# Moving spatial weight tiles and the bias out of the last pass of a two-layer attention and gMLP kernel, and lending it idle PSUM banks

## The chip, the cores and the metric

The kernel runs on one core of a Trainium2 chip. The metric is the device time of one execution in microseconds (us), lower is better.

## The reference, cut to what matters

Two layers, each an attention with 32 query heads of width 16 over one shared key and value head, and then a gMLP. The batch is 1, there are 2048 tokens, the model width is 512, the MLP width is 1792.

```python
def _A_ref(x, wq, wk, wv, wo):             # attention, one k/v head
    q = (x @ wq) -> heads                  # 32 heads x 16
    scores = q @ k.T * 16 ** -0.5          # 2048 x 2048 per head, not causal
    return (softmax(scores) @ v) -> merged @ wo

def _B_ref(x, w_in, w_sp, b_sp, w_out):    # gMLP
    z = gelu(x @ w_in)                     # 2048 x 1792
    z1 = z[..., :896]
    z2 = layernorm(z[..., 896:])
    g = einsum('ts,bsf->btf', w_sp, z2) + b_sp[None, :, None]   # mixes over tokens
    return (z1 * g) @ w_out

for _ in range(2):
    x = x + _A_ref(layernorm(x), ...)
    x = x + _B_ref(layernorm(x), ...)
```

What matters here: `g` at any token needs `z2` of all 2048 tokens, so it cannot be finished before the attention of the last token is done. And the keys of layer 1 need the finished `x` of layer 0. So at the end of each layer there is a stretch with nothing left of that layer's attention to overlap with.

## The kernel before: the parts that the change touches

The kernel is a Python list scheduler. It builds all operations with dependences, priorities and assumed durations, and it writes one fixed order of instructions for each engine: PE (matmul), ACT, DVE, POOL and SP (DMA issue). Each engine's program is that order, with waits on semaphores; the order is settled before the kernel runs.

A "job" is a group of matmuls into one PSUM bank and the evictions that release it. Six of the eight banks belong to attention, two are "side" banks for all other work:

```python
self.chunks = [512, 512, 512, 256, 128, 128]        # tokens per attention chunk
self.passes = [(0, 4, 0), (4, 8, 1), (8, 12, 2)]    # spatial partial sums: token tiles s0..s1, started after chunk ci
self.s_fin = 12                                     # the final pass takes tiles 12..16
self.ring = [(0, 3), (3, 2)]                        # attention scores: banks 0-2 and 3-4
self.pvb = 6                                        # P x V
sc = self.sc = Sched([5, 7])                        # side banks
```

Attention is shared by two engines. ACT does the exponential of most score blocks ("A" blocks). DVE does it for the others ("D" blocks) by a chain of seven vector operations. A further stream sends filler matmuls that multiply by zero, to keep PE busy enough for its clock.

After each chunk's attention comes its MLP (layernorm, transposes, `w_in`, gelu, layernorm). The spatial product is summed over token tiles in passes; a pass that is not the last evicts into the partial sum `gp` in SBUF. The final pass starts after the last chunk. It is the routine below (`...` marks cuts, and a call with `<-` in it is a DMA in short form, destination first):

```python
def spatial(self, s0, s1, layer, final):
    acc = s0 > 0
    pr = 2.0 if final else 4.0
    ...
    for tc in range(8):                              # 8 blocks of 256 output tokens
        sl = self.ws_n % (NWS // 4)                  # four weight slots, used in turn
        ld = self.dma(... self.wsT[:, 4 * sl:4 * sl + s1 - s0, :] <- w_sp.T[s0:s1, tc * 256:(tc + 1) * 256] ...)
        ...
        for f0 in range(0, NF, 2):                   # 7 groups of 128 features, two to a bank
            ...
            for i, f in enumerate(fs):
                todo = []
                if final:
                    todo.append(("b", None))         # bias: an 8-row matmul
                if final:
                    todo.append(("g", None))         # gp: identity matmul
                todo += [("w", w) for w in ws]       # one matmul for each token tile
        ...
            if kind == "b":
                ins = e.matmul(o_, self.ident[0:8, tc:tc + 1].to_broadcast([8, P]), self.b8[:, :], ...)
            elif kind == "g":
                ins = e.matmul(o_, self.ident[:], self.gp[:, tc, f, :], ...)
            else:
                ins = e.matmul(o_, self.z2n[:, w[0], f * 128:(f + 1) * 128], self.wsT[:, w[1], :], ...)
        # not final: DVE copies or adds the bank to gp
        # final:     DVE multiplies by z1 -> hT; then 14 matmuls with w_out for 2 token tiles,
        #            X is added by DVE; in layer 0 the keys of layer 1 are built from it,
        #            in layer 1 X is stored to the output
```

The softmax here doesn't subtract the row's maximum and nothing guards it: scores larger than these inputs give would overflow.

## Time and profile before

| | before |
|---|---|
| median of the first three executions | 2031.84 us (2019.77 to 2033.57) |
| span of the profiled execution | 2028.9 us |
| mean granted PE clock | 0.928 |
| ACT busy | 1745.4 us |
| DVE busy | 1804.6 us |
| PE busy | 1683.5 us |

The page of the profile gives the busy time of each engine and then, in forty equal slices of 50.7 us, the busy share of each in tenths, with the granted PE clock. Four of its lines:

```profile
PE 1683.5 (83%) x17285; PEld 674.8 (33%) x17285; DVE 1804.6 (89%) x3287; ACT 1745.4 (86%) x1528; POOL 58.7 (3%) x105
DVE  7999999999999999985459999999998999989654
ACT  7999999999998999991369999999999999999700
PEclk9999998989897898799988979989899999979799
```

ACT and DVE are full almost everywhere. There are two holes in ACT: around slices 19 to 21, and in the last two or three. The averages over the span hide this. I call those stretches the seams.

To read them, I cut the span by events of the trace: layer 0's attention from 20 us to its last exponential on ACT; the head, from there to the first matmul of the final pass; the final pass and the keys of layer 1, to the last copy of a key; and the same for layer 1, with the output in place of keys. Columns of the windows view: window, its length, then busy us and instructions of PE, PE weight loads, DVE, ACT and POOL, then the granted clock, the DMA share and GB/s.

```profile
20.00:909.00 889.00, 729.67 (x7904) 275.52 (x7902) 846.63 (x1536) 852.60 (x733) 15.17 (x26) 0.93 0.12 31
909.00:933.00 24.00, 20.12 (x198) 13.96 (x195) 14.93 (x32) 6.20 (x11) 1.58 (x4) 1.00 0.28 83
933.00:1051.00 118.00, 109.98 (x763) 56.62 (x761) 55.86 (x108) 40.35 (x46) 7.54 (x16) 0.96 0.19 53
1051.00:1910.60 859.60, 708.23 (x7642) 262.02 (x7642) 816.30 (x1471) 827.36 (x711) 16.35 (x22) 0.92 0.03 10
1910.60:1944.60 34.00, 26.70 (x214) 17.92 (x214) 19.37 (x42) 9.32 (x18) 3.32 (x8) 0.85 0.35 99
1944.60:2029.00 84.40, 79.61 (x501) 42.79 (x500) 35.69 (x56) 0.00 (x0) 0.00 (x0) 1.00 0.27 80
```

In the two attention windows ACT is busy 96% of the time. In the four other windows, 260 us together, it is not; PE is the busiest engine there, at 94% in the last one (79.61 of 84.40 us).

The timeline of PE shows what it does in the last window. Columns: start, duration (ends are modelled, so durations overlap; differences of starts are the reliable reading), engine, line, operation, output and inputs, shapes, count. This is one of eight blocks, from the second set of seven output matmuls of the block before it to its own first output matmul:

```profile
2007.31 1.67 PE L1005 MATMUL ps_all<-E 128*128 128x512 bf16 x7
2008.92 0.28 PE L952 MATMUL ps_all<-b_12,ident 8*128 8x256 bf16 x1
2009.13 0.28 PE L955 MATMUL ps_all<-gp,ident 128*128 128x256 bf16 x1
2009.25 0.60 PE L957 MATMUL ps_all<-wsT,z2n 128*128 128x256 bf16 x4
2009.78 0.28 PE L952 MATMUL ps_all<-b_12,ident 8*128 8x256 bf16 x1
...
2013.82 1.69 PE L1005 MATMUL ps_all<-E 128*128 128x512 bf16 x7
```

One group of six matmuls repeats every 0.86 us (2008.92 to 2009.78). The 8-row bias matmul is followed by its neighbour only after 0.21 us, and it starts 0.21 us after the last of the four weight matmuls before it. The identity matmul is followed after 0.12 us, and weight matmuls are 0.109 us apart. The Trainium skill, "TensorE: Matmul & The Clock Gate", section Back-to-back issue gap, gives N/2.4 + 2.5 ns for an isolated warm matmul of N columns, 109 ns for 256; the trace agrees. The block period, from one block's output matmuls at 2004.71 us to the next one's at 2013.82, is 9.11 us.

One group of the whole program. Columns: line, engine, operation, tiles and shapes, count, busy us, mean ns of one, idle time before them and its releaser. It is the exponential on ACT (two other groups: the first DVE operation on a D block counts 519, the filler matmuls 821):

```profile
L1173 ACT ACTIVATE Pa<-ps_all 128x1536 bf16<-128x1536 f32 (+1 forms) x1431 | 1638.9, 1304 | 72.6 <-PE ps_all L1429 64.7
```

### The profile page before, as it was taken

What the parts mean: (1) busy time and instruction counts of PE and PEld (TensorE: products, weight loads), DVE (VectorE), ACT (ScalarE), POOL (GpSimd) and SP (SyncE); (2) the same over time, 40 slices, a digit from 0 to 9 for tenths busy, and PEclk for the clock granted to TensorE, in tenths of its full rate; (3) what the DMA queues carried; (4) which work ended last, traced back from release to release, by engine and by line L of the source; (5) the groups of instructions that cost most, each with busy time, mean ns of one, the idle gap of its engine ahead of it and who ended that gap; (6) DMA issues with size and microseconds to landing.
All of it is one profiled execution on the core that took longest, in us unless ns stands there. A gap on an engine that the chain in (4) does not pass through costs nothing.

```text
span 2028.9 us, 41252 instructions
## 1 busy us (share of the span) xinstructions
PE 1683.5 (83%) x17285; PEld 674.8 (33%) x17285; DVE 1804.6 (89%) x3287; ACT 1745.4 (86%) x1528; POOL 58.7 (3%) x105
## 2 busy tenths in 40 slices
PE   7777788978798887879987787898888977878799
PEld 3111222422241334555431112233222413345454
DVE  7999999999999999985459999999998999989654
ACT  7999999999998999991369999999999999999700
POOL 2000000000000000000000000000000000000000
PEclk9999998989897898799988979989899999979799
DMA  9700000000010000012110000000000100000132
GB/s 271 182 1 1 1 1 30 28 5 1 29 32 1 2 2 25 3 44 73 35 39 1 1 1 1 19 22 22 1 1 24 32 6 2 2 20 3 44 94 78
DMA packets 104057, 59.82 MB, mean 29 GB/s; under 512 B 40121, under 2 KB 101313, under 8 KB 103873
## 3 DMA queue, kind: packets, MB, share of 16 engines
q1 hardware_dynamic: 102288, 56.64, 10.0%
q8 instruction: 137, 2.24, 0.4%
q10 hardware_dynamic: 1584, 0.56, 0.1%
q14 instruction: 48, 0.39, 0.1%
HBM read 30.97 MB, written 17.83 MB: 24 GB/s over the span
## 4 chain that ended last, share of the span: by engine, by line
DVE 32%; PE 32%; ACT 25%; issue 9%; DMA 1%; POOL 1%; SPq 0%; ACTq 0%
ACT Pa L1173 22%; PE ps_all L1429 8%; PE ps_all L957 7%; DVE E L1340 6%; DVE Pd L1378 5%; PE ps_all L1241 5%; DVE E L1373 3%; DVE E L1376 3%; DVE E L1367 3%; PE ps_all L1005 3%; PE ps_all L1416 2%; PE ps_all L853 2%; DVE E L1369 2%; DVE E L1370 2%; PE ps_all L704 1%
## 5 line engine op out<-in xcount | busy, mean ns | idle before, releaser
L1173 ACT ACTIVATE Pa<-ps_all 128x1536 bf16<-128x1536 f32 (+1 forms) x1431 | 1638.9, 1304 | 72.6 <-PE ps_all L1429 64.7
L1429 PE MATMUL ps_all<-qs,kT 32*128 32x512 bf16 (+2 forms) x6144 | 597.1, 331 | 262.1 <-ACT Pa L1173 240.4
L1429 PEld LDWEIGHTS ps_all<-qs,kT 32*128 32x128 bf16 x6144 | 177.1, 95 | 751.2 <-ACT Pa L1173 660.8
L1340 DVE TENSOR_SCALAR E<-ps_all 128x512 int32<-128x512 f32 x519 | 351.3, 682 | 25.7 <-PE ps_all L1429 23.7
L1241 PE MATMUL ps_all<-Pa,V 128*32 128x512 bf16 (+2 forms) x5366 | 352.8, 331 | 2.7 <-DVE oT L727 1.6
L1378 DVE SCALAR_TENSOR_TENSOR Pd<-E 128x1024 uint16<-128x1024 int32 (+1 forms) x260 | 315.3, 1213 | 0.8
L957 PE MATMUL ps_all<-wsT,z2n 128*128 128x256 bf16 x1792 | 252.5, 275 | 12.1 <-DVE gp L973 7.0
L1416 PE MATMUL ps_all<-wo_r,zero 128*128 128x512 bf16 (+2 forms) x821 | 218.4, 376 | 0.0
L1241 PE MATMUL ps_all<-Pd,V 128*32 128x512 bf16 (+2 forms) x778 | 196.4, 334 | 0.0
L957 PEld LDWEIGHTS ps_all<-wsT,z2n 128*128 128x128 bf16 x1792 | 159.8, 98 | 83.2 <-issue 21.1
L1373 DVE TENSOR_TENSOR E<-E 128x1024 f16<-128x1024 f16 (+1 forms) x260 | 177.3, 682 | 3.0
L1376 DVE TENSOR_TENSOR E<-E 128x1024 f16<-128x1024 f16 (+1 forms) x260 | 177.1, 681 | 2.3
L1367 DVE TENSOR_SCALAR E<-E 128x1024 f16<-128x1024 uint16 (+1 forms) x260 | 176.7, 681 | 1.1
L1241 PEld LDWEIGHTS ps_all<-Pa,V 128*32 128x32 bf16 x5366 | 104.0, 99 | 133.8 <-issue 115.8
L1370 DVE TENSOR_SCALAR E<-E 128x1024 f16<-128x1024 f16 (+1 forms) x260 | 108.4, 417 | 2.1
L1369 DVE TENSOR_SCALAR E<-E 128x1024 f16<-128x1024 f16 (+1 forms) x260 | 108.3, 416 | 1.5
L1416 PEld LDWEIGHTS ps_all<-wo_r,zero 128*128 128x128 bf16 x821 | 65.4, 104 | 105.9 <-issue 90.4
L973 DVE TENSOR_TENSOR gp<-ps_all,gp 128x512 bf16<-128x512 f32 (+1 forms) x128 | 77.9, 617 | 20.1 <-PE ps_all L957 19.4
L984 DVE TENSOR_TENSOR E<-ps_all,z1s 128x512 bf16<-128x512 f32 x64 | 39.9, 624 | 51.8 <-PE ps_all L957 48.5
L704 PE MATMUL ps_all<-xnTA,wq_pad 128*128 128x512 bf16 (+2 forms) x384 | 77.9, 324 | 3.8 <-DVE E L1340 1.8
L853 PE MATMUL ps_all<-xnTB,w_in_r 128*128 128x512 bf16 (+2 forms) x336 | 69.2, 326 | 6.8 <-DVE z1s L861 3.0
L832 PE MATMUL ps_all<-w_in_r,xnTB 128*128 128x448 bf16 x256 | 65.1, 366 | 7.4 <-DVE E L1340 3.6
(74 smaller groups left out, 1115.4 us busy)
## 6 DMA issues: line engine op xcount, KB each, us to landing
wsT<-wsT_scratch SPq DMA_DIRECT2D x64, 256.0 KB, 2.8
wsT_scratch<-gp SPq DMA_DIRECT2D x16, 512.0 KB, 3.6
z1s<-z_scratch SPq DMA_DIRECT2D x16, 448.0 KB, 4.1
z_scratch<-z1s SPq DMA_DIRECT2D x6, 896.0 KB, 4.0
X<-in_A_x_dram SPq DMA_DIRECT2D x8, 256.0 KB, 6.2
out_dram<-X SPq DMA_DIRECT2D x16, 128.0 KB, 1.7
w_in_r<-in_B_w_in_dram SPq DMA_DIRECT2D x1, 1792.0 KB, 10.8
E<-in_B_w_out_dram SPq DMA_DIRECT2D x2, 896.0 KB, 5.5
```

The costliest lines, as they stand in the source:

```text
L957: ins = e.matmul(o_, self.z2n[:, w[0], f * 128:(f + 1) * 128], self.wsT[:, w[1], :], start=st, stop=sp_)
L1173: return e.activation(k.Pa[:, base:base + n, :], k.b32(b0, n).rearrange("p (k q) -> p k q", k=n), ACTF.Exp, scale=SCALE)
L1241: ins = e.matmul(k.b32(k.pvb)[32 * j:32 * j + 32, 0:n], k.V[:, kt, 32 * j:32 * j + 32], b.slot[:, s * n:(s + 1) * n], tile_position=(0, 32 ...
L1340: return k.sc.op("dve", lambda e: e.tensor_scalar(k.eI[:, s, 512 * i:512 * (i + 1)], k.b32(j.bank.idx)[:, 0:512], C_LOG2, C_BIAS, op0=ALU. ...
L1367: return lambda e: e.tensor_scalar(out, a, m, None, op0=ALU.mult)
L1369: return lambda e: e.tensor_scalar(out, a, b, None, op0=ALU.add)
L1370: return lambda e: e.tensor_scalar(out, a, m, b, op0=ALU.mult, op1=ALU.add)
L1373: o4 = sc.op("dve", lambda e: e.tensor_tensor(q, u, w, ALU.mult), d_sb(n, 0.521e-3), [o3], pr)
L1376: o6 = sc.op("dve", lambda e: e.tensor_tensor(q, q, u, ALU.mult), d_sb(n, 0.521e-3), [o5], pr)
L1378: o7 = sc.op("dve", lambda e: e.scalar_tensor_tensor(po.bitcast(U16), I, 2.0 ** -9, q, op0=ALU.mult, op1=ALU.add), d_sb(n, 1.042e-3), [o6] ...
L1416: ins = e.matmul(k.b32(k.pvb)[:, 0:n], k.zero[:], k.wo_r[:, 0, 0:n], start=False, stop=False)
L1429: ins = e.matmul(self.b32(bank)[:, s * n:(s + 1) * n], self.kT[32 * j:32 * j + 32, kt * 128:(kt + 1) * 128], self.qs[32 * j:32 * j + 32, g ...
```

## The change

Its intent is to shorten the seams. The parts:

1. The final pass takes two token tiles instead of four; the passes become (0,8), (8,12) and (12,14), and the final one 14 to 16.
2. The bias is added in the first pass, under attention, instead of the final one.
3. The partial sum `gp` is fp16 instead of bf16, with an fp16 identity.
4. Once attention of a layer has no more use for its PSUM banks, they are lent to the side jobs, and reclaimed when the next layer's attention starts.
5. The queries, and the `z1` halves, of small chunks share one bank and one eviction.
6. The MLP of small chunks has a higher priority (1.0, and 0.3 for the last, against 3.0 and 1.5), and the last chunk's `z1` has a buffer of its own.
7. DVE takes no D block in the last six units of a layer, nor while an urgent side job waits for a bank.

The diff, cut to its core (helpers for lending, the packing code of queries and `z1`, and bookkeeping are left out):

```diff
-        self.passes = [(0, 4, 0), (4, 8, 1), (8, 12, 2)]
-        self.s_fin = 12
+        self.passes = [(0, 8, 1), (8, 12, 2), (12, 14, 3)]
+        self.s_fin = 14
...
-        self.gp = sb([P, 8, NF, 256], BF16, "gp")
+        self.gp = sb([P, 8, NF, 256], FP16, "gp")
...
+    def lend(self, key, idxs, o):
+        self.lent[key] = []
+        for i in idxs:
+            b = Bank(i)
+            b.free_at, b.rel = o.vis, [o]
+            self.lent[key].append(b)
+            self.banks.append(b)
...
-        pr = 1.5 if last else 3.0
+        pr = PR_LAST if last else (PR_SMALL if g.ci >= 3 else 3.0)     # 0.3, 1.0
...
-        for f in range(NF):                    # z1: one bank and one eviction for each feature group
+        per = 512 // n                         # now 512 // n groups share one
+        for f0 in range(0, NF, per):
...
-        pr = 2.0 if final else 4.0
+        pr = 2.0 if final else (2.5 if s1 > 12 else 4.0)
...
+        if final:                              # the final weights as four DMAs into the two slots
+            for i in range(2):
+                t_ = self.wsT[:, 8 * i:8 * i + 8, :].rearrange("p s t -> p (s t)")
+                for k, (c0, c1) in enumerate(((512, 2048), (0, 512))):
+                    war = self.ws_wide[i] if k == 0 else self.last_ws[i]
+                    ldf.append(self.dma(... t_[:, c0:c1] <- self.ws_dv[:, s0 + i, c0:c1], war ...))
...
-                    if final:
+                    if not acc:
                         todo.append(("b", None))
...
-        if sc.bank_free() > t:
+        if sc.bank_free() > t or any(o.first and o.prio < URGENT and o.ready <= t for o in sc.ready["pe"]):
             return None
...
-            if un.grp.layer != layer:
+            if un.grp.layer != layer or u >= self.limit(layer):        # ENDX = 6 units
                 return None
```

The weights of the passes under attention now go through two slots of up to eight tiles, where there were four slots of four.

## The prediction

> **What bounds the kernel now.** By the page's engine totals, ACT (1745 us, 86%) and DVE (1805 us, 89%) are full, except (the 40 slices) in the middle and at the end. Cut into windows (us):
>
> | stage | before | ACT busy | predicted |
> |---|---|---|---|
> | attention, layer 0 (from 20) | 889 | 96% | 899 |
> | head: last exp to final pass | 24 | 26% | 21 |
> | final spatial pass + layer-1 keys | 118 | 34% | 73 |
> | attention, layer 1 | 860 | 96% | 875 |
> | head | 34 | 27% | 24 |
> | final pass, output | 84 | 0 | 47 |
>
> So about 260 us, the "seams", are not ACT-bound. In the last pass PE is the limit (79.6 of 84.4 us busy). The timeline shows each of 8 column blocks taking 9.1 us: seven groups of 0.86 (bias, partial sum, four weight matmuls), 14 output matmuls at 0.22. The 8-row bias matmul has 0.21 us before and after it, where a normal 256-column matmul takes 0.107 (the Trainium skill, "TensorE: Matmul & The Clock Gate", Back-to-back issue gap: N/2.4+2.5 ns = 109; the trace agrees). The 34 us head holds small chunks' MLPs, a 2.9 us spill wait and half of the (8,12) pass.
>
> **What changes**, by counts in the two programs' orders:
> - Final pass: a group falls from six matmuls to three. Totals stay; 112 weight matmuls and 56 biases per layer move under attention. Estimate per block: 7 x 0.32 + 14 x 0.217 = 5.3 us against 9.1. Lent banks (two serve side work now) remove stalls. DVE needs about 3.9 us per block, a z1 reload 4.1 double-buffered, so PE stays the limit.
> - Middle: PE work of pass, keys, queries and early fills is about 95 us of 118 before, 63 after by the same durations; DVE about 56. Attention done inside is unchanged (55 score blocks before the last keys).
> - Heads: small-chunk MLPs run earlier; the LN–MLP–gelu–LN chain (about 20 us) remains, beside 46 and 116 leftover weight matmuls and a late 128x512 weight load (3 us).
> - Attention: DVE takes 494 score blocks instead of 519, so ACT 3602 instead of 3577, at 0.458 us: +11.5 us. A gelu with its table loads leaves the tail: +4.4. In layer 1's 128-token chunks PE work rises from 91 to 105 us beside some 118 of ACT; they already ran at 91% ACT, clock 0.85. I allow 9 us more ACT waiting. Warm-up matmuls fall from 821 to 625.
>
> **Critical path.** The predicted column sums to -70 us: the final passes carry it, attention gives back 25.
>
> **Prediction: 1960 us, 8 in 10 between 1936 and 1988.** Chances: faster by over 2% 0.93, within 2% 0.06, slower 0.01.
>
> **What would show each step.** Last pass 5.3 us per block, PE over 90% busy; it starts about 24 us after the last exp; in the middle 95–100 us from layer 0's last exp to the last key copy (142 before); ACT exp time up about 11 us; ACT at least 88% busy in the last two chunks; few PE waits on DVE evictions in the seams.
>
> **What would make it wrong.** The last pass bound by z1 reloads queued behind output stores, or by DVE; the middle bound by the LN-to-key chain, with DVE and PE nearly even; PE starving ACT in the small chunks, attention growing 20–40 us; fp16 identity matmuls slower than bf16; the (12,14) sums (one 0.69 us DVE add per four matmuls of 0.43 us) holding back the last head.

## The result, and the profile after

The changed kernel took 1977.81 us (median of four, 1975.98 to 1979.22) against 2031.86 us before (2019.77 to 2033.57). Its outputs were correct. Ratios here are the mean time of one kernel's fast runs over that of the other's of the same rounds, so they are not quite the ratio of the quoted medians: 0.9746, 95% interval 0.9707 to 0.9785. A second set of runs gave 1979.68 us, ratio 0.974 (0.9713 to 0.9766). The prediction said 1960 us with a range of 1936 to 1988: faster, as predicted, and 18 us less so than the central figure.

The four lines of the page (a slice is 49.4 us now):

```profile
PE 1643.6 (83%) x17089; PEld 653.6 (33%) x17089; DVE 1747.8 (89%) x3141; ACT 1761.0 (89%) x1532; POOL 57.3 (3%) x106
DVE  7999999999989999784779999999998898997855
ACT  7999999999999999995479999999999999999940
PEclk9988898999999998998998988987898999989999
```

The windows, cut by the same events:

```profile
20.00:910.10 890.10, 750.87 (x8084) 283.96 (x8082) 819.40 (x1462) 860.63 (x741) 16.27 (x26) 0.95 0.12 32
910.10:935.00 24.90, 12.22 (x108) 8.48 (x109) 11.07 (x23) 6.44 (x9) 1.56 (x4) 0.81 0.50 137
935.00:1013.00 78.00, 74.38 (x567) 41.65 (x567) 52.13 (x106) 37.79 (x42) 7.50 (x16) 0.97 0.13 36
1013.00:1892.60 879.60, 732.00 (x7807) 270.75 (x7807) 800.30 (x1416) 840.13 (x720) 15.44 (x26) 0.92 0.04 13
1892.60:1925.60 33.00, 20.69 (x181) 14.79 (x175) 20.79 (x43) 6.45 (x10) 1.56 (x4) 0.85 0.42 123
1925.60:1974.20 48.60, 44.63 (x280) 28.07 (x280) 28.39 (x48) 0.00 (x0) 0.00 (x0) 0.96 0.33 100
```

Stage by stage (us):

| stage | before | predicted | after | after minus predicted |
|---|---|---|---|---|
| attention, layer 0 | 889.0 | 899 | 890.1 | -8.9 |
| head, layer 0 | 24.0 | 21 | 24.9 | +3.9 |
| final pass and keys | 118.0 | 73 | 78.0 | +5.0 |
| attention, layer 1 | 859.6 | 875 | 879.6 | +4.6 |
| head, layer 1 | 34.0 | 24 | 33.0 | +9.0 |
| final pass and output | 84.4 | 47 | 48.6 | +1.6 |

The seams lost 75.9 us (260.4 to 184.5) and attention gained 21.1 (1748.6 to 1769.7), together 54.8. The difference of the two spans is 54.7; the 0.1 is rounding of the cuts.

The last pass runs as predicted. Its timeline of one block:

```profile
1942.07 3.19 PE L1079 MATMUL ps_all<-E 128*128 128x512 bf16 x14
1945.09 0.38 PE L1026 MATMUL ps_all<-wsT,z2n 128*128 128x256 bf16 x2
1945.31 0.27 PE L1024 MATMUL ps_all<-gp,ident_3 128*128 128x256 f16 x1
...
1947.38 3.19 PE L1079 MATMUL ps_all<-E 128*128 128x512 bf16 x14
```

The period is 5.31 us (1942.07 to 1947.38), against the 5.3 predicted, and a group of three matmuls takes 0.33 us. The fp16 identity matmul is followed after 0.11 us, so it is no slower than the bf16 one. PE does not wait on evictions there.

The same group of the whole program (the DVE group counts 494, the fillers 625):

```profile
L1249 ACT ACTIVATE Pa<-ps_all 128x1536 bf16<-128x1536 f32 (+1 forms) x1442 | 1654.4, 1297 | 72.5 <-PE ps_all L1518 66.8
```

DVE takes 25 score blocks fewer, and ACT's exponentials take 15.5 us more (1638.9 to 1654.4; I had predicted 11.5). Within attention, ACT's idle time went from 36.4 to 29.5 us in layer 0 and from 32.2 to 39.5 in layer 1.

What did not go as predicted are the heads. They are as long as before, although they hold less work: in layer 1's head PE is busy 20.7 of 33.0 us. The PE timeline of that head, where the bracket at the end of a row is idle time and what ended it:

```profile
1896.69 1.02 PE L843 MATMUL ps_all<-wo_r,onT 128*128 128x512 bf16 x4
1904.05 5.32 PE L1026 MATMUL ps_all<-wsT,z2n 128*128 128x256 bf16 x26 [6.33 <-DMA wsT<-wsT_scratch]
1909.20 0.39 PE L619 MATMUL ps_all<-ident,xn 128*128 128x128 bf16 x4
...
1917.32 1.70 PE L1026 MATMUL ps_all<-wsT,z2n 128*128 128x256 bf16 x14 [0.73 <-DMA wsT<-wsT_scratch]
1921.22 2.02 PE L1026 MATMUL ps_all<-wsT,z2n 128*128 128x256 bf16 x14 [2.21 <-DMA wsT<-wsT_scratch]
1925.62 0.39 PE L1024 MATMUL ps_all<-gp,ident_3 128*128 128x256 f16 x1 [2.37 <-DMA wsT<-wsT_scratch]
```

The last projection of attention is issued at 1896.69. What must follow is the chain of the last 128 tokens: layernorm, transposes, `w_in`, gelu, layernorm, final pass. But in PE's fixed order, matmuls of pass (12,14) come before the transposes (`ident,xn` at 1909.20), and they wait 6.33 us for a 128 KB weight load. Then three further loads hold PE up for 0.73, 2.21 and 2.37 us. The sum is 11.6 us. Layer 0's head has one such wait of 5.54 us, at 921.12. The queue of SP shows why the loads were late (columns as above; SPq is SP's queue of DMA issues):

```profile
1893.53 0.43 SPq L964 DMA_DIRECT2D E<-in_B_w_out_dram  x1
1894.01 1.37 SPq L998 DMA_DIRECT2D z1s<-z_scratch  x2
1895.42 3.15 SPq L979 DMA_DIRECT2D wsT<-wsT_scratch  x1
1898.61 11.58 SPq L990 DMA_DIRECT2D wsT<-wsT_scratch  x4
...
1919.05 0.36 SPq L990 DMA_DIRECT2D wsT<-wsT_scratch  x1
```

The queue holds 896 KB of `w_out`, two reloads of `z1` (448 KB each) and wide final weights (384 KB each) in the same few us. The wide load at 1895.42 held the queue for 3.15 us, and the small loads (L990) stand behind it. It was not held by PE reading its slot: counted back from the end, all spatial matmuls from 1894.61 on belong to pass (12,14), which does not touch this part of the slot. More likely it was what the queue already held; in layer 0 a load of only 128 KB behind the same burst was held for 2.87 us (914.09). From issue to landing the first two small loads took 5.4 and 5.1 us there, against 2.2 us in the median of this stretch.

The three later waits have another cause, the two slots. A load into a slot can only be issued when PE has finished with what is in it. The load at 1919.05 follows the end of the matmuls of 1917.32 (at 1919.02) at once, and PE, which has nothing else to do in its order, waits until it has landed, 2.2 us later; the final load at 1923.28 and the one at 1915.09 came the same way. So 6.3 of the 11.6 us are put down to the crowded queue, and 5.3 to slots that are refilled only when PE has left them.

After such waits PE also runs at half rate for a while. In the final pass of layer 1, the first five groups of three start 0.61 to 0.64 us apart, later ones 0.33 (this is the 0.39 us duration in the last line above; normal ones show 0.27). That is about 2 us lost in each layer. The Trainium skill, "TensorE: Matmul & The Clock Gate", section What's actually happening, describes a clock gate that throttles PE after an idle window of about 3.4 us and is released by about 3.4 us of activity; its section Back-to-back issue gap gives N/1.2 ns for a cold matmul, 213 ns for 256 columns. The trace agrees with the cost and the release: 0.64 us for three is 213 ns each, and PE, which began again at 1925.62, was slow until about 1929.3. It does not agree with the idle window: the granted clock was 1.00 from 1913.4 to 1922.0 and 0.50 from 1922.5 us on, and PE's waits in between were of 0.73 and 2.21 us.

### The profile page after: what moved, and what is told of

Its sections match the earlier page's. It is cut to its first block, busy times and chain, and to the rows that moved or that the text cites. A ratio compares the mean times of both kernels' runs of the same rounds, so it can differ in the third digit from the quotient of the medians.

```text
span 1974.2 us, 40665 instructions
## 1 busy us (share of the span) xinstructions
PE 1643.6 (83%) x17089; PEld 653.6 (33%) x17089; DVE 1747.8 (89%) x3141; ACT 1761.0 (89%) x1532; POOL 57.3 (3%) x106
## 3 DMA queue, kind: packets, MB, share of 16 engines
q8 instruction: 135, 2.21, 0.5%
## 4 chain that ended last, share of the span: by engine, by line
PE 37%; ACT 29%; DVE 21%; issue 11%; DMA 1%; POOL 1%; ACTq 0%; SPq 0%; POOLq 0%
ACT Pa L1249 26%; PE ps_all L1518 10%; PE ps_all L1026 8%; PE ps_all L1325 6%; DVE E L1429 4%; DVE Pd L1467 3%; PE ps_all L1505 3%; PE ps_all L1079 3%; DVE E L1462 2%; DVE E L1465 2%; PE ps_all L874 2%; DVE E L1456 2%; ACT z2n L920 1%; PE ps_all L746 1%; DVE E L1459 1%
## 5 line engine op out<-in xcount | busy, mean ns | idle before, releaser
L1249 ACT ACTIVATE Pa<-ps_all 128x1536 bf16<-128x1536 f32 (+1 forms) x1442 | 1654.4, 1297 | 72.5 <-PE ps_all L1518 66.8
L1429 DVE TENSOR_SCALAR E<-ps_all 128x512 int32<-128x512 f32 x494 | 335.3, 684 | 39.4 <-PE ps_all L1518 37.0
L1467 DVE SCALAR_TENSOR_TENSOR Pd<-E 128x1024 uint16<-128x1024 int32 x248 | 300.3, 1211 | 1.0
L1026 PE MATMUL ps_all<-wsT,z2n 128*128 128x256 bf16 x1792 | 277.4, 280 | 20.0 <-DMA wsT<-wsT_scratch 14.8
L1505 PE MATMUL ps_all<-wo_r,zero 128*128 128x512 bf16 (+2 forms) x625 | 195.5, 414 | 0.0
L1462 DVE TENSOR_TENSOR E<-E 128x1024 f16<-128x1024 f16 x248 | 168.8, 681 | 3.3
L1465 DVE TENSOR_TENSOR E<-E 128x1024 f16<-128x1024 f16 x248 | 168.9, 681 | 2.5
L1456 DVE TENSOR_SCALAR E<-E 128x1024 f16<-128x1024 uint16 x248 | 168.9, 682 | 1.5
L1042 DVE TENSOR_TENSOR gp<-ps_all,gp 128x512 f16<-128x512 f32 (+1 forms) x128 | 76.4, 616 | 35.5 <-PE ps_all L1026 35.3
L1459 DVE TENSOR_SCALAR E<-E 128x1024 f16<-128x1024 f16 x248 | 103.4, 417 | 2.6
L1458 DVE TENSOR_SCALAR E<-E 128x1024 f16<-128x1024 f16 x248 | 103.6, 418 | 2.2
L769 DVE CAST oT<-ps_all 128x512 bf16<-128x512 f32 (+2 forms) x96 | 48.6, 506 | 14.5 <-PE ps_all L1325 12.5
```

Source lines behind the costliest of these rows:

```text
L1249: return e.activation(k.Pa[:, base:base + n, :], k.b32(b0, n).rearrange("p (k q) -> p k q", k=n), ACTF.Exp, scale=SCALE)
L1429: return k.sc.op("dve", lambda e: e.tensor_scalar(k.eI[:, s, 512 * i:512 * (i + 1)], k.b32(j.bank.idx)[:, 0:512], C_LOG2, C_BIAS, op0=ALU. ...
L1456: return lambda e: e.tensor_scalar(out, a, m, None, op0=ALU.mult)
L1459: return lambda e: e.tensor_scalar(out, a, m, b, op0=ALU.mult, op1=ALU.add)
L1462: o4 = sc.op("dve", lambda e: e.tensor_tensor(q, u, w, ALU.mult), d_sb(n, 0.521e-3), [o3], pr)
L1465: o6 = sc.op("dve", lambda e: e.tensor_tensor(q, q, u, ALU.mult), d_sb(n, 0.521e-3), [o5], pr)
```

## The experiments

Twelve runs were made, in three groups of four (ten new kernels, and two repeats); the kernel before ran beside each group, with medians of 2031.44, 2031.47 and 2031.92 us. Every one gave a correct result. Times below are medians with lowest and highest, and the ratio to before with its 95% interval. The lines "seams" and "attention" are cut from each run's one trace by the same events as above. As a measure of noise: two traces of the changed kernel agree in each seam within 0.4 us, but differ by 5.6 and 3.2 us in the two attentions.

### The changed kernel again

No edit; it repeats the result within the first group, as the base for the other runs.

> The changed kernel itself, as the yardstick on this chip for the runs beside it: 1974 to 1980 us, ratio to before 0.974 within 0.003. Stages as in its first trace: heads 25 and 33 us, final pass with keys 78, last final pass with output 49.

1979.68 us (1972.31 to 1985.28), ratio 0.974 (0.9713 to 0.9766). Stages: 895.7, 25.2, 78.0, 882.8, 33.3, 48.4 us. The seams repeat; the whole difference in span of this slower execution lies in the attentions.

### The bias alone, in the kernel before

```diff
# kernel before
-                    if final:
+                    if not acc:
                         todo.append(("b", None))
...
-                if final:
+                if not acc:
                     deps.append(self.l_b)
```

> The kernel before with one part of the change alone: the bias matmul moves from the final pass to the first partial sum, which runs under attention. Theory: the last pass is PE-bound and each bias costs 0.33 us there, so its block period falls from 9.1 to about 6.9 us and the two final passes lose about 18 us each: 1995 us, ratio about 0.982. Rival: with two PSUM banks the pass is bound by evictions once the matmuls shrink, and only half of it comes: 2013 us.

2020.49 us (2008.45 to 2031.0), ratio 0.9936 (0.99 to 0.9972). In its trace the seams shrank by 36.1 us, the 36 of the theory, but only 30.6 of it in the final passes (202.4 to 171.8), the rest in the heads (58.0 to 52.5). But the time fell by only 11 to 13 us, because attention of layer 1 took 882.0 us instead of 859.6, and that of layer 0 894.3 instead of 889.0. So seam time taken away is not time gained. The block period was 7.57 us and not the 6.9 of the pure matmul sum; the timeline shows PE waiting on DVE at each block:

```profile
1962.14 0.61 PE L957 MATMUL ps_all<-wsT,z2n 128*128 128x256 bf16 x4 [0.24 <-DVE E L984]
1965.05 1.68 PE L1005 MATMUL ps_all<-E 128*128 128x512 bf16 x7 [0.35 <-DVE X L1010]
```

With the bias gone, evictions through two banks become part of the limit. Why attention of layer 1 gave 22 us back is open. The windows show only where: ACT's busy time there is the same (829.3 us against 827.4), so it is idle time of ACT, and its waits for score matmuls of PE rose from 26.9 to 43.6 us. It is not simply the cost of 56 bias matmuls under attention, as the next run shows.

### The bias back in the final pass, in the changed kernel

```diff
# changed kernel
-                    if not acc:
+                    if final:
                         todo.append(("b", None))
```

> The changed kernel with the bias matmul put back into the final pass, all else as it is. Theory: each 8-row bias matmul costs about 0.33 us there (its own 0.107 and 0.21 lost), 56 of them per layer, so the last pass goes from 5.3 to about 7.6 us per block and the whole kernel is 30 to 37 us slower (about 2010), while attention gains nothing because ACT bounds it. Rival: the 0.21 us gaps hide behind the matmuls' weight loads or evictions, the bias costs its 0.107 only: 12 us slower.

2019.13 us (2010.62 to 2022.82), ratio 0.9932 (0.9905 to 0.996): 39 us more than the changed kernel in the same group, slightly above the expected range. The final passes took 95.9 and 67.9 us (78.0 and 48.6 with the bias early), 37 us together; attention was 888.7 and 882.3, as with the bias early. So in the changed kernel attention carries the bias for nothing that these traces resolve. The block period was 7.53 us:

```profile
1974.12 3.19 PE L1079 MATMUL ps_all<-E 128*128 128x512 bf16 x14
...
1981.65 3.19 PE L1079 MATMUL ps_all<-E 128*128 128x512 bf16 x14
```

The difference to 5.31, divided by seven, is 0.317 us for one bias matmul, of 8 rows, in a stream where a full-row one costs 0.109. I had expected 0.33. The Trainium skill, "TensorEngine Tiling (Array Packing)", section Key Properties, says that "Changing tiling mode (not just tile) drains the TensorE". This could be such a change, but no run here shows that it is. The bias also differs from its neighbours in its first operand, one column repeated 128 times, and no run tells the two apart.

This one move is worth about 39 of the 52 us between the two kernels in this group, when it is taken away last; taken alone first (the run above), it is worth 11. The parts of the change are not additive.

### No lent banks

```diff
# changed kernel
     def lend(self, key, idxs, o):
+        return
         self.lent[key] = []
```

> The changed kernel, but no attention bank is lent; side work keeps its two banks in the seams. My theory: a bank is held for its matmuls (0.65 us for a pair of groups, 1.5 for an output row) plus about 1 us of eviction and semaphores, so a column block holds two banks for about 11.3 us in sum, 5.6 us each, and the last pass goes from 5.3 to 5.6-6.5 us per block: 3 to 10 us more per seam, 6 to 20 us in all (1980 to 1998). Rival A, PE is the only limit: no change, within 3 us. Rival B, the banks carry most of the gain: over 30 us slower.

1993.68 us (1993.26 to 2000.37), ratio 0.9815 (0.9792 to 0.9839): 14 to 15 us slower than the changed kernel, within the expectation. The block period was 7.0 us instead of 5.31, more than expected, with the same two waits in each block:

```profile
1957.65 0.28 PE L1024 MATMUL ps_all<-gp,ident 128*128 128x256 f16 x1 [0.46 <-DVE E L1053]
1960.56 1.68 PE L1079 MATMUL ps_all<-E 128*128 128x512 bf16 x7 [0.57 <-DVE X L1084]
```

The final passes took 83.9 and 59.6 us (78.0 and 48.6 with lending). With two banks, PE must wait for the multiplication by `z1` and for the addition of X; with eight, it runs ahead. The Trainium skill, "Perfetto Trace Analysis", section Matmul Optimizations, advises to "Ensure all 8 PSUM banks are being leveraged"; here that is worth 1.7 us in 7.0 of each block. One thing went the other way: layer 0's head was 19.2 us instead of 24.9, since with fewer banks fewer spatial matmuls had been placed ahead of the transposes in PE's order.

### The old priorities of small chunks

```diff
# changed kernel
-PR_LAST = 0.3
-PR_SMALL = 1.0
+PR_LAST = 1.5
+PR_SMALL = 3.0
```

> The changed kernel with the old priorities of the MLP of small chunks (3.0, and 1.5 for the last). Theory: chunk 3's and 4's MLP and gelus fall behind the (12,14) and (8,12) sums and partly into the last head, so the heads grow by 5 to 15 us each, and in the last 120 us of attention ACT's busy share falls from 98% toward the 91 to 94% of before: 15 to 25 us slower (about 2000). Rival: the 98% comes from fewer score blocks on DVE (fewer chains to wait for), not from the order of the MLP: ACT stays at 98% and only the heads grow, under 12 us.

1981.93 us (1976.6 to 1984.9), ratio 0.9753 (0.9724 to 0.9781): 2 to 3 us slower, which the intervals do not tell from nothing. The heads became longer (31.6 and 35.1 us, against 24.9 and 33.0), and the other stages stayed within 2 us. ACT's busy share in the last 120 us of each attention stayed at 0.99 and 0.98. So the theory that the priorities keep ACT full in the small chunks falls. The outcome is the rival's; its reason, fewer score blocks on DVE, is not shown by it, and the run with the old DVE rules below speaks for it in one layer at most. The priorities of part 6 are worth little here.

### A final pass of four tiles, no (12,14)

```diff
# changed kernel
-        self.passes = [(0, 8, 1), (8, 12, 2), (12, 14, 3)]
-        self.s_fin = 14
+        self.passes = [(0, 8, 1), (8, 12, 2)]
+        self.s_fin = 12
# and the final weights by block, through the two slots, as in the other passes
```

> The changed kernel with the (12,14) partial sum undone: the final pass takes four token tiles again, loaded per column block as before; bias first, lent banks and priorities stay. Theory: five matmuls per group instead of three make the block period about 6.9 us, 12 us more in each final pass (+24), but 64 DVE additions and the weight-load stalls in the heads go away (heads about 20 and 24 us, -14) : a net of 5 to 12 us slower than the changed kernel, so this part is nearly a wash as built. Rival: the narrowing is worth its full matmul count, 20 us or more slower.

1985.09 us (1982.7 to 2004.6), ratio 0.9791 (0.9756 to 0.9826): slower than the changed kernel by 5 us by medians and 10 by means (across two groups), one of the six runs being at 2004.6. The final passes grew by 12.1 and 12.5 us (period 6.84 us: 14 more matmuls at 0.109). But the heads fell to 19.8 and 19.7 us:

```profile
920.40:940.10 19.70, 7.64 (x65) 4.23 (x65) 4.55 (x11) 6.44 (x9) 1.56 (x4) 0.71 0.05 12
1900.10:1919.80 19.70, 7.63 (x66) 4.22 (x67) 4.55 (x11) 6.44 (x9) 1.56 (x4) 0.79 0.04 12
```

These are the windows of the two heads, with the same columns as above: about 65 matmuls each. No engine is busy for even 40% of the time, and PE, DVE, ACT and POOL add up to 20.2 us in 19.7, as they would if they worked nearly one after another. This is the bare chain of the last 128 tokens, 19.7 us (I had put it at about 20). It is not a floor: with a granted clock of 0.94 in place of 0.71, layer 0's head without lent banks took 19.2 us. The run shows that (12,14) wins 24.6 us in the final passes and loses 18 of them in the heads.

### The weights of the last four tiles, loaded early

The buffer of the transposed normalised input of attention (`xnTA`) is idle from the time a layer's last queries are made until the next layer's keys. Its 16 KB in each partition hold the weights of token tiles 12 to 15 whole, so neither pass (12,14) nor the final pass has to load any in the head.

```diff
# changed kernel
+        own = final or nst == 2
+        if own and not final:
+            rd = [o for p in range(8) for o in self.xnTA_read[p]]
+            self.ldx = [self.dma(... self.xnTA[:, i, :] <- self.ws_dv[:, s0 + i, :],
+                                 rd + self.ws_st[s0 + i:s0 + i + 1], ...) for i in range(4)]
...
-                lds = [ldf[1], ldf[3]] if tc < 2 else [ldf[0], ldf[2]]
-                ws = [(s, self.wsT[:, 8 * (s - s0) + tc, :]) for s in range(s0, s1)]
+                lds = self.ldx[s0 - 12:s1 - 12]
+                ws = [(s, self.xnTA[:, s - 12, tc * 256:(tc + 1) * 256]) for s in range(s0, s1)]
```

> The changed kernel with the spatial weights of the last four token tiles loaded early and whole into the xnTA tile, which is idle once a layer's queries are made, so neither the (12,14) sums nor the final pass waits for a weight load in a head. Theory: the heads lose the DMA waits seen on PE (5.5 us in the middle, 6.3 and about 5 at the end): heads about 20 and 22 us, 12 to 17 us faster than the changed kernel (about 1962). Rival: the chain of layer norm, MLP, gelu, layer norm sets the heads and the waits were hidden beside it: under 5 us.

1971.13 us (1965.33 to 1982.19), ratio 0.9707 (0.9679 to 0.9735). The heads fell to 21.3 and 21.9 us, by 3.6 and 11.1; the final passes stayed (76.7 and 48.1). The same kernel was run again in the third group:

> The early-weights kernel again, as the yardstick for the filler version on this chip: 1965 to 1980 us, ratio to before 0.971 within 0.003, heads 21 and 22 us.

1968.31 us (1961.01 to 1974.51), ratio 0.968 (0.9656 to 0.9705), with heads of 21.3 and 21.9 us again. Its PE timeline of layer 1's head:

```profile
1898.49 0.40 PE L619 MATMUL ps_all<-ident,xn 128*128 128x128 bf16 x4 [2.25 <-DVE xn L610]
1899.57 2.69 PE L874 MATMUL ps_all<-w_in_r,xnTB 128*128 128x448 bf16 x8 [0.69 <-ACT xnTB L628]
1911.10 0.39 PE L1017 MATMUL ps_all<-gp,ident 128*128 128x256 f16 x1 [6.62 <-DVE z2n L941]
```

There is no wait on a DMA left. PE waits for the chain itself: for the layernorm (`xn`) and, 6.62 us, for gelu and the second layernorm (`z2n`). So the late loads caused the long heads: 14.7 us in the trace, of which the times show 7 to 12, less than the 12 to 17 expected. Two things limit this. The run takes away the crowded queue and the shared slots together, so it does not say what each is worth. And it moves work: layer 1's head now holds 128 matmuls instead of 181, since some of pass (12,14) could run before the last exponential. In layer 0 the head holds more matmuls than before (178, not 108), and is still shorter. This is the best version. It beats the kernel before by 3.0 to 3.2% and the changed kernel by 0.3 to 0.6%; the interval of its second set (up to 0.9705) does not touch that of the changed kernel (from 0.9713), that of its first set overlaps a little.

### The old rules for DVE's share

```diff
# changed kernel
-ENDX = 6
-URGENT = 1.25
+ENDX = 0
+URGENT = -9.0
```

> The changed kernel without the two new limits on DVE's share of the exps (no block in the last 6 units of a layer; none while an urgent job waits for a bank): DVE takes 516 score blocks by count instead of 494. Theory: ACT bounds attention, so 22 blocks at 0.458 us less make it about 10 us faster in attention, and the heads lose a few us of it to late DVE chains: 3 to 8 us faster. Rival: the limits keep ACT fed in the small chunks (98% busy) and without them it falls to 93%: 5 us or more slower.

1985.46 us (1982.17 to 1992.95), ratio 0.9779 (0.9749 to 0.9808): 6 to 8 us slower than the changed kernel (by medians and by ratios). DVE took 516 blocks again; attention was 884.4 and 879.5 us, 5.7 less, which is no more than two traces of one kernel differ by, and the same. But the heads were 31.0 and 39.6 us, since late D chains stand in DVE's order among the additions to `gp` and the last layernorm. The expectation that it would be faster falls. Here it pays to leave ACT with more exponentials at the end. I did not test the two rules one by one.

### More filler in the kernel before

```diff
# kernel before
-WARM = 250.0
+WARM = 800.0        # filler matmuls 821 -> 1208
```

> The kernel before, one constant changed: the filler matmuls that keep the PE clock up are set to aim at 800 columns above the scheduler's threshold instead of 250 (1208 fillers by count instead of 821). Theory: in the last 120 us of each attention ACT idles because PE, nearly full, falls to the slower clock (granted 0.85 to 0.91 there, ACT 91 to 96% busy; 0.97 and 98% in the changed kernel); more filler raises the clock above 0.95 and ACT above 97% there, and the kernel gets 8 to 20 us faster. Rival: the fillers are themselves what delays the score matmuls; more of them lowers ACT's share and the kernel gets 5 us or more slower.

2016.84 us (2006.79 to 2023.69), ratio 0.992 (0.9894 to 0.9946), 15 to 16 us faster. The time is as expected, the reason is not. The mean granted clock rose from 0.926 to 0.958 in the mean of the timed runs. Attention of layer 0 fell by 20 us in the trace, and that of layer 1 rose by 7. But in the small chunks, which this run was made for, ACT's share did not rise in both layers. The last 120 us of each attention (first the kernel before, then this run):

```profile
789.00:909.00 120.00, 101.04 (x2370) 64.53 (x2363) 108.12 (x237) 114.88 (x99) 3.98 (x8) 0.91 0.06 16
1790.60:1910.60 120.00, 101.57 (x2323) 63.02 (x2311) 108.89 (x232) 109.63 (x94) 5.07 (x6) 0.85 0.03 9
```

```profile
768.60:888.60 120.00, 101.59 (x2424) 65.41 (x2427) 105.99 (x235) 111.97 (x97) 5.85 (x8) 0.93 0.06 19
1778.00:1898.00 120.00, 100.68 (x2387) 64.04 (x2393) 103.10 (x226) 112.46 (x98) 5.34 (x8) 0.90 0.06 16
```

ACT was busy 111.97 and 112.46 us of 120 with clocks of 0.93 and 0.90, against 114.88 and 109.63 with 0.91 and 0.85. The changed kernel has 118.04 and 117.55, with a clock of 0.97 in both.

### No filler in the 128-token chunks, in the kernel before

```diff
# kernel before, filler stream
-        if u >= len(k.units) or k.units[u].first or not k.dex_on:
+        if u >= len(k.units) or k.units[u].first or not k.dex_on or k.units[u].grp.n == 128:
             return None
```

> The kernel before without any filler matmul in the 128-token chunks (152 fewer). Theory (the clock): granted clock in the last 120 us of each attention falls below 0.85 and ACT's share below 91%, 3 to 10 us slower. Rival (fillers delay the score matmuls): ACT's share rises above 96% and the kernel is faster.

2042.99 us (2037.13 to 2048.28), ratio 1.0049 (1.0028 to 1.0069), 10 us slower. The clock in the last 120 us of the attentions fell to 0.67 and 0.75, and yet ACT was busy 111.03 and 111.25 us there, hardly less than in the kernel before. The loss lies in layer 0's head, 44.5 us instead of 24.0. That head holds 285 matmuls instead of 198, and 16.9 us of ACT's work instead of 6.2: without the fillers the scheduler wrote another order, in which MLP work slid behind the last exponential. Together the two filler runs show that the granted clock does not by itself decide how full ACT is in the small chunks. Neither of my two explanations holds.

### Early weights and more filler together

```diff
# early-weights kernel
-WARM = 250.0
+WARM = 800.0
```

> The changed kernel with early weights (as e5) and the filler target 800. Theory: e5 shortened the two heads by 15 us in its trace but lost about 9 us of ACT time in the last 120 us of attention at a clock of 0.94 to 0.96; with more filler the clock there is 0.98 or more and ACT 98% busy, so it is 5 to 12 us faster than e5 alone (1958 to 1965). Rival: fillers take PE time from side work and delay it into the heads: no gain over e5.

1974.01 us (1964.96 to 1976.67), ratio 0.9708 (0.9685 to 0.9732), against 0.968 for the early-weights kernel of the same group. The mean clock was 0.955 against 0.935, and nothing came of it. What helped the kernel before by 16 us did not help here; the two gains do not add.

### What was not run

The fp16 partial sum, the shared banks and evictions of small chunks, the own buffer of the last chunk's `z1`, and each of the two DVE rules by itself were not isolated. An early-weights version with a weight buffer of its own, instead of the idle one, did not fit into SBUF beside the rest.

## Why the prediction was right, and where it was off

The prediction was right in its class, and the time lies within its range. The central figure was 18 us too low (15 in the profiled span). Point by point:

- "Estimate per block: 7 x 0.32 + 14 x 0.217 = 5.3 us against 9.1." Right: 5.31 us in the trace. Of the 3.8 us saved, 7 x 0.317 = 2.2 is the bias (measured by putting it back) and 1.5 the two tiles fewer (measured by the four-tile run).
- "Lent banks ... remove stalls. ... PE stays the limit." Right: without lending the block takes 7.0 us, with waits on DVE at two places in each block.
- "Middle: PE work ... is about 95 us of 118 before, 63 after." The direction was right, the size of this term was off. The windows show PE busy 110.0 us before and 74.4 after. The fall of 35.6 is near the 32 that I had counted, but I had taken the rest of the 118 us, 23 us, for stalls of which the change would remove 13; there were only 8 us without PE work. So the stage fell by 40 us instead of 45.
- "Heads: ... the LN–MLP–gelu–LN chain (about 20 us) remains, beside 46 and 116 leftover weight matmuls and a late 128x512 weight load (3 us)." The chain is right: 19.7 us when nothing else is there. The load term was the step that failed: PE waited 5.5 us in layer 0 and 11.6 us in layer 1, there at four loads and not at one. I had costed one load alone. I had not asked what stands in front of it in the DMA queue, nor when PE leaves the slot that it goes to, nor seen that PE's fixed order puts the waiting matmuls ahead of the transposes, so that a late load delays the chain and not just itself. Loading the weights early took 14.7 us out of the heads, which is more than the 12.9 us by which they exceeded the prediction. That the loads were the cause is shown; how it divides between queue and slots is not.
- "Attention: ... +11.5 us ... +4.4 ... 9 us more ACT waiting." The sum was 25 and 21.1 was measured, but the parts differ. Exponentials cost 15.5 us more, not 11.5. ACT's other waits did not grow by 9: they fell by 7 in layer 0 and rose by 7 in layer 1. That the sum came close is partly luck.
- "ACT at least 88% busy in the last two chunks." It was 98% in the last 120 us of both attentions, where the kernel before had 96 and 91%. I had expected PE's extra work to starve ACT there. Why the opposite happened stays open: it is neither the priorities (old ones: still 99 and 98%), nor lending, nor the old DVE rules alone (99 and 94%), nor simply the clock (the two filler runs). Versions with nearly the same instructions differ by several per cent there (early weights: 95 and 94%).
- "few PE waits on DVE evictions in the seams": right for the final passes. In the heads, DVE's additions to `gp` and the layernorm share one order, as the old DVE rules showed by making both heads 6 us longer.

So the gain did not come from attention, which is the larger part of the time and gave back 21 us, but from 76 us less in the seams: in the traces they grow by 41 us when the bias is put back, by 14 without the lent banks, and by 6 with four tiles.

## What to carry to other kernels

Cut the span by events before costing a change: an engine that is 86% busy on average, as ACT was, can be at 96% for most of the time and idle in the seams, and it was the seams that this change shortened. When a list scheduler writes fixed orders, a late DMA can cost more than its own time, because work that could go on stands behind it (two heads lost 14.7 us to loads that I had costed at 3); ask for each load in a tail what the queue already holds and when its slot comes free, and put tail data into a buffer that has gone idle, early. Measure the worth of a part both ways, alone and as the last to be removed: the bias move was worth 11 us in the one way and 39 in the other, and the seams shrank by much the same in both (36 and 41 us). What differed was attention, which gave 28 us back in the one way only; why, no run shows.

## What the Trainium skill lacked or had wrong

- "TensorE: Matmul & The Clock Gate", section Back-to-back issue gap, calls N/2.4 + 2.5 ns the gap of isolated matmuls, and gives lower or higher figures for a sustained stream: about 131 ns at N=512 and 81 ns at N=128 (its part on the 2.5 ns has the formula back to back as well). In these traces a sustained stream follows the formula: 14 matmuls of 512 columns took 3.02 us (1942.07 to 1945.09 us), 216 ns each, and 28 of 128 columns took 1.56 us (1911.80 to 1913.36 us), 56 ns each.
- The same page has no cost for a matmul with few rows among full-row ones; its closing table says only that a single one with K=32 takes as long as one with K=128. With 8 rows and 256 columns it cost 0.317 us in each group, where a full-row one costs 0.109. "TensorEngine Tiling (Array Packing)", section Key Properties, says that a change of tiling mode drains the engine, without a figure; whether this is the cause, no run shows.
- "TensorE: Matmul & The Clock Gate", section What's actually happening, has the gate throttle after an idle window of about 3.4 us. Here the granted clock fell to 0.50 at 1922.5 us after waits of 0.73 and 2.21 us.
- The same page prices throttled PE time alone (Terms: the time times 1 - K/N); it does not say what a higher granted clock is worth in a kernel where other engines bind too. Over the 103 timed executions here, runs of one and the same kernel were 7.9 us faster for each 0.01 of mean granted clock (correlation -0.90 after the mean of each kernel and group is taken out; a correlation, no cause). Between kernels this does not hold: raising the clock from 0.926 to 0.958 by filler gave 16 us, not 25, and from 0.935 to 0.955 in the early-weights kernel gave nothing.
- "DMA: Bandwidth & Descriptors", section Queues, rings and completion order, says that descriptors of a ring are consumed in order. It gives no figure for a small load behind a burst: in layer 1's head 128 KB landed in 2.2 us in the median, and in 5.1 and 5.4 us behind some 2.5 MB in the same queue (896 + 2 x 448 + 2 x 384 KB); in layer 0's head it took up to 7.0 us.
- "Perfetto Trace Analysis", section Matmul Optimizations, advises all eight PSUM banks, without a figure. Here two side banks instead of eight cost 1.7 us in each 5.3 us block.
- No page tells how to find work that stands behind a waiting instruction in a fixed engine order. Here one head had 11.6 us of waits on loads, and was 11.1 us shorter without them.
